# Mask rows of the second batch (batch one, counted from zero) by engine copies instead of DMAs, a selector made on GpSimd, and a new order of all work, in a fused block-sparse attention and SoLU feed-forward kernel

## The chip, the cores and the metric

The kernel runs on one core of a Trainium2 chip. The metric is the device time of one execution in microseconds; the time before is the median of three runs. A core has five engines with queues of their own: TensorE (PE, with PEld for its weight loads), VectorE (DVE), ScalarE (ACT), GpSimd (POOL) and SyncE (SP, which here issues nearly all DMAs). Each works through its own row of instructions in order and waits on semaphores for the others.

## The reference

Attention with a block mask over 4 batches, 8 heads, 768 positions and 64 columns per head; its output, as 3072 tokens of 512, goes through a feed-forward layer of width 1024 with a SoLU activation and a layer norm.

```python
scores = scale * np.matmul(q, k.transpose(0, 1, 3, 2))
mask = np.abs(blk_i - blk_j) <= 1          # blocks of 32
mask = mask | (blk_i == 0) | (blk_j == 0) | (blk_i == 23) | (blk_j == 23)
mask[qb rows, kb columns] = True           # for the 3 sampled blocks kb of each block row qb
attn = softmax(np.where(mask, scores, -1e9))
x = np.matmul(attn, v)                     # 3072 x 512, heads side by side
h = x @ w_in                               # 3072 x 1024
solu = h * softmax(h)
out = ((solu - mu) / np.sqrt(var + 1e-06) * g_ln) @ w_out
```

## The kernel before

Heads are taken in pairs (`pr`, 4 per batch). For each batch `b`, `kT` and `qT` hold k and q transposed: 64 rows of values and, below them, 24 **mask rows** (`MC = slice(64, 88)`). On k's side these say to which of the 24 blocks a key belongs, on q's side they hold minus 30000 for each block that a query may not see, so that one matmul of 88 rows gives the masked score. There are two buffers of each, for even and odd batches. The mask rows are the same for every batch and pair, and are made once.

*Opening.* Batch zero's k and q are loaded, cast (`cast2` to `cast6`), transposed on TensorE into `abank` (`turned`) and evacuated; its mask rows come along in the same transposition, from columns that affine selects (`own`) and small operations on VectorE (`bar`, ending in `bar_b`) have written. The **selector** `selp` (24 x 768) is block membership transposed: six transpositions on TensorE (`selp_tp`) and one copy on ScalarE (`selp`); with it `mask2` and `mcol` place `bar_b` in q's mask. For batch one, two DMAs (`m1dma`) copy all four pairs of mask rows from `kT[0]` and `qT[0]` to `kT[1]` and `qT[1]`, 288 KB each. They wait for all evacuations and for all casts of `w_in` (`castw`), because `w_in` is staged in the memory of `kT[1]` and `qT[1]`.

*Later batches.* `crossed` casts k and q (into `kb`, `qb`), transposes them by DMA (`cross_kq`, into `kx`, `qx`, shown as `kc` and `qx`) and **splits** the result by head into `kT` or `qT` with two copies of 64 rows each.

*Attention.* `attend(b, t, pr)` works on 256 queries and two heads: three groups of four score matmuls (L561) into one of two `sbank` buffers, each followed by one exponential of 128 x 1024 on ScalarE (L568), then 24 matmuls with `va` (L581) into one of two `mbank` buffers, a reciprocal (L590) and a normalisation (L593) into `x`.

*Feed-forward.* For each of 24 tiles of 128 tokens: x is transposed by DMA (`cross_x`) or on TensorE, 8 matmuls with `w_in` (L643), exponential with its sum (L666), product (L669), statistics (L676, L679), `u` transposed by DMA (`cross_u`), 8 matmuls with `w_out_sb` (L759), and scaling by `rs` (L767, L769). `rs` comes from three small operations on GpSimd (`z2` L682, `vr` L685, `rs` L718). `w_out` is prepared once: eight scalings by g (`wg`, L439), their column sum on TensorE (`cs`), `wbar` on ScalarE (L451) and eight products on VectorE (`wo`, L453).

*Order.* Nothing is scheduled at run time. The functions only list operations with what they depend on. `ORDER`, a list of numbers, gives the sequence in which all are issued and so each engine's row; `ENGINES` moves single operations of choice (casts, splits, scalings) to another engine. `SPARES` lists matmuls on constants (L823) that compute nothing that is used; they are placed by `ORDER` as well.

## Time and profile before

| | |
|---|---|
| median of 3 runs | 211.07 us (210.95 to 211.72) |
| profiled execution, its own time | 210.25 us |
| its span, first to last instruction | 208.5 us |
| busy TensorE / VectorE / ScalarE / GpSimd | 200.3 / 138.8 / 179.4 / 84.2 us |
| first score matmul, first exponential | 8.03, 8.67 us after the start |
| first score of batch one | 49.28 us |
| data moved by DMA | 43.19 MB |

The profiled execution is a single one and 0.8 us below the median. A busy TensorE is not a TensorE at its peak: neighbouring matmuls overlap, and the shown length of one is longer than its place in the row. In the rows "idle before" names the time in which an engine stood before this instruction, and "<-" what ended it.

### The profile page before, as it was taken

What the parts mean: (1) busy time and instruction counts of PE and PEld (TensorE: products, weight loads), DVE (VectorE), ACT (ScalarE), POOL (GpSimd) and SP (SyncE); (2) the same over time, 40 slices, a digit from 0 to 9 for tenths busy, and PEclk for the clock granted to TensorE, in tenths of its full rate; (3) what the DMA queues carried; (4) which work ended last, traced back from release to release, by engine and by line L of the source; (5) the groups of instructions that cost most, each with busy time, mean ns of one, the idle gap of its engine ahead of it and who ended that gap; (6) DMA issues with size and microseconds to landing.
All of it is one profiled execution on the core that took longest, in us unless ns stands there. A gap on an engine that the chain in (4) does not pass through costs nothing.

```text
span 208.5 us, 5748 instructions
## 1 busy us (share of the span) xinstructions
PE 200.3 (96%) x2282; PEld 142.0 (68%) x2313; DVE 138.8 (67%) x306; ACT 179.4 (86%) x230; POOL 84.2 (40%) x158
## 2 busy tenths in 40 slices
PE   8999999999999999999799999999999999999993
PEld 4798876756667768566566767666767758666452
DVE  5586689999887555757676864754755565485840
ACT  3599999998999999999599998989989898876683
POOL 4235398185540647316640731683320211001271
PEclk9999999999999999999999999999999999999999
DMA  5999995999999998999899989995393314672534
GB/s 142 336 358 347 384 361 123 205 226 287 211 222 327 311 189 208 254 263 286 230 299 228 233 185 251 207 257 126 101 127 99 63 19 104 151 105 53 122 134 152
DMA packets 71736, 43.19 MB, mean 207 GB/s; under 512 B 53348, under 2 KB 67180, under 8 KB 71660
## 3 DMA queue, kind: packets, MB, share of 16 engines
q1 hardware_dynamic: 71672, 42.81, 84.9%
q8 instruction: 18, 0.29, 0.6%
q14 instruction: 10, 0.08, 0.1%
q10 hardware_dynamic: 36, 0.00, 0.0%
HBM read 23.07 MB, written 6.29 MB: 141 GB/s over the span
## 4 chain that ended last, share of the span: by engine, by line
PE 73%; DVE 12%; DMA 7%; ACT 3%; issue 2%; SPq 1%; ACTq 0%
PE sbank L561 22%; PE mbank L759 15%; PE hbank L643 14%; PE mbank L581 13%; DMA qx<-qb 4%; DVE w_out_sb L453 3%; PE abank L477 3%; ACT ex L568 2%; DMA xT<-x 2%; DVE u L669 2%; PE tbank L643 2%; PE sbank L823 2%; DVE x L593 1%; DMA out_dram<-ot 1%; DVE w_in_sb L295 1%
## 5 line engine op out<-in xcount | busy, mean ns | idle before, releaser
L568 ACT ACTIVATE ex<-sbank 128x1024 bf16<-128x1024 f32 x144 | 141.0, 1025 | 15.7 <-PE sbank L561 14.2
L561 PE MATMUL sbank<-qT,kT 88*128 88x256 bf16 x576 | 81.5, 272 | 0.5 <-DVE qT L295 0.3
L561 PEld LDWEIGHTS <-kT 88*128 88x128 bf16 x576 | 52.7, 97 | 19.2 <-issue 0.9
L759 PE MATMUL mbank<-w_out_sb,uT 128*128 128x512 bf16 x175 | 45.0, 379 | 0.8 <-DVE w_out_sb L453 0.3
L581 PEld LDWEIGHTS <-ex 128*128 128x128 bf16 x1152 | 40.8, 97 | 7.0 <-issue 1.3
L581 PE MATMUL mbank<-va,ex 128*128 128x65 bf16 x1152 | 42.3, 193 | 1.4 <-DVE x L593 1.3
L643 PE MATMUL hbank<-w_in_sb,xT 128*128 128x512 bf16 x157 | 41.9, 378 | 1.4 <-DMA xT<-x 0.3
L669 DVE TENSOR_TENSOR u<-hbank,e 128x1024 bf16<-128x1024 f32 x22 | 26.8, 1216 | 19.6 <-ACT e L666 15.7
L676 DVE BATCH_NORM_STATS2 bs<-u 128x6 f32<-128x512 bf16 x44 | 29.2, 679 | 0.2
L643 PEld LDWEIGHTS <-xT 128*128 128x128 bf16 x192 | 18.2, 97 | 15.0 <-DMA xT<-x 0.8
L759 PEld LDWEIGHTS <-uT 128*128 128x128 bf16 x184 | 17.6, 97 | 14.6 <-issue 0.8
L590 DVE RECIPROCAL r<-mbank 128x4 f32<-128x4 f32 x48 | 8.3, 175 | 25.7 <-PE mbank L581 25.5
L666 ACT ACTIVATE e<-hbank 128x1024 bf16<-128x1024 f32 x22 | 22.5, 1024 | 1.3 <-PE hbank L643 1.3
L685 POOL TENSOR_SCALAR vr<-z,mv 128x1 f32<-128x1 f32 x22 | 5.8, 266 | 39.0 <-DVE mv L679 38.0
L593 DVE TENSOR_TENSOR x<-mbank,r 128x256 bf16<-128x256 f32 x48 | 19.7, 415 | 0.8
L718 POOL TENSOR_TENSOR rs<-vr,neg_half 128x1 f32<-128x1 f32 x24 | 13.8, 579 | 0.8
L295 POOL COPY qT<-kc 64x768 bf16<-64x768 bf16 x10 | 8.9, 889 | 11.7 <-DMA kc<-qb 6.1
L769 DVE TENSOR_SCALAR ot<-mbank,rs 128x512 f32<-128x512 f32 x13 | 9.7, 745 | 5.7 <-PE mbank L759 3.1
L682 POOL TENSOR_TENSOR z<-z 128x1 f32<-128x1 f32 x22 | 4.7, 212 | 20.1 <-ACT e L666 19.7
L295 POOL CAST kb<-kst 128x768 bf16<-128x768 f32 x7 | 6.2, 892 | 15.3 <-DMA kst<-in_k_dram 8.8
L295 POOL COPY kT<-kc 64x768 bf16<-64x768 bf16 x13 | 11.0, 844 | 2.6 <-DMA kc<-kb 2.2
L295 POOL CAST va<-vst 128x768 bf16<-128x768 f32 x8 | 6.6, 827 | 7.4 <-DMA vst<-in_v_dram 7.3
(110 smaller groups left out, 165.5 us busy)
## 6 DMA issues: line engine op xcount, KB each, us to landing
vst<-in_v_dram SPq DMA_DIRECT2D x16, 384.0 KB, 5.0
out_dram<-ot SPq DMA_DIRECT2D x23, 256.0 KB, 2.4
kst<-in_k_dram SPq DMA_DIRECT2D x15, 384.0 KB, 4.7
qst<-in_q_dram SPq DMA_DIRECT2D x12, 384.0 KB, 5.3
w_out_f<-in_moe_w_out_dram SPq DMA_DIRECT2D x2, 1024.0 KB, 8.4
qst<-in_q_dram SPq DMA_DIRECT2D x4, 256.0 KB, 5.9
kT<-in_moe_w_in_dram SPq DMA_DIRECT2D x2, 512.0 KB, 5.5
qT<-in_moe_w_in_dram SPq DMA_DIRECT2D x2, 512.0 KB, 9.4
```

Of the source, the lines that this page charges most:

```text
L295: (nc.vector if o.eng == "DVE" else nc.gpsimd).tensor_copy(out=dst, in_=src)
L561: nc.tensor.matmul(s[:, m, :], kT[i][0:KR, pr, jc, hh, :], qT[i][0:KR, pr, 2 * t : 2 * t + 2, hh, :], start=(m % 2 == 0), stop=(m % 2 == 1))
L568: exs.append(op("exp", "ACT", lambda o, so=so: nc.scalar.activation(out=exb[o.slot], in_=sbank[so.slot], func=ACT.Exp, scale=scale), [so], ...
L581: nc.tensor.matmul(acc(o)[:, qt, hh, :], exb[exs[n].slot][:, m, qt * P : (qt + 1) * P], va[i][:, 2 * pr + hh, jc, :], start=first, stop=(n ...
L593: nrm = op("norm", "DVE", lambda o: nc.vector.tensor_tensor(out=xb[x_of[b, t].slot][:, :, 2 * pr * D : (2 * pr + 2) * D].rearrange("p a (h ...
L643: nc.tensor.matmul(d, xTb[xt[0].slot][:, qt, c, :], w_in_sb[n][:, c, :], start=(c == 0), stop=(c == KD - 1))
L666: zs = op("silu_e", "ACT", lambda o: nc.scalar.activation(out=eb[o.slots["e"]], in_=hb(), func=ACT.Exp, accum_out=zb[o.slots["z"]][:, 0:1] ...
L669: us = op("mult", "DVE", lambda o: nc.vector.tensor_mul(out=ub[o.slot], in0=hb(), in1=eb[zs.slots["e"]]), [zs], take="u", last_of=[(hs[0], ...
L676: bs.append(op("stats", "DVE", lambda o, n=n: nc.vector.bn_stats(out=bsb[(bs[0] if bs else o).slot][:, n, :], in_=ub[us.slot][:, w(o, n)]) ...
L718: rs = op("rs", "POOL", lambda o: nc.gpsimd.tensor_tensor(out=rsb[o.slot], in0=vrb[vr.slot], in1=neg_half, op=ALU.pow), [vr, c2], take="rs ...
L759: nc.tensor.matmul(mbank[m0.slot], uTb[ut[0].slot][:, KF // 2 * n + f, :], w_out_sb[n][:, f, :], start=(n == 0 and f == 0), stop=(n == 1 a ...
L769: nc.vector.tensor_scalar(out=otb[o.slot], in0=mbank[os_[0].slot], scalar1=rsb[rs.slot], scalar2=None, op0=ALU.mult)
```

## The change

- `selp_tp` and its copy go. Four affine selects on GpSimd write `selp` directly, in two parts (two of the six chunks, then four).
- The two `m1dma` go. In their place stand eight copies `mrow` of 24 x 1536, one for each pair of k and q, on GpSimd or VectorE; each waits only for batch zero's first pair and for the casts of that part of `w_in` that lies in its place (`staged`). The splits of batch one wait for the same part instead of all of `w_in`.
- `kown` becomes in part an order (`after`) instead of a dependence. `iota_f`, `samp_f`, and of the feed-forward `z2` and `vr`, may now run on another engine.
- `SPARES`, `ENGINES` and `ORDER` are new throughout.

```diff
 SPARES = (
-    (512, 'a'), (256, 'a'), (128, 'm'), (512, 'a'), (512, 'a'), (512, 'm'), (512, 'a'), (512, 'm'), (256, 'm'),
...
+    (512, 's'), (512, 's'), (512, 's'), (512, 's'), (512, 's'), (128, 's'), (128, 's'), (128, 's'), (128, 's'),
...
-    st = op("selp_tp", "PE", selp_tp, [own, mids], take="m")
-    sels = op("selp", "ACT", lambda o: copy(
-        o, selp.rearrange("a c p -> a (c p)"), mbank[st.slot].bitcast(BF16)[0:NB, 0 : NCH * P]), [st], last_of=[st])
+    sels = []
+    for c0, c1 in ((0, 2), (2, NCH)):
+        a = op(f"selp{c1 - c0}", "POOL", lambda o, c0=c0, c1=c1: nc.gpsimd.affine_select(
+            out=selp[:, c0:c1], in_=nc.const_aps.tensor(1.0, (NB, c1 - c0, P), BF16), compare_op=ALU.is_ge,
+            fill=0.0, base=c0, channel_multiplier=-BLK, pattern=[[1, c1 - c0], [NCH, P]]))
+        sels.append(op(f"selp{c1 - c0}", "POOL", lambda o, c0=c0, c1=c1: nc.gpsimd.affine_select(
+            out=selp[:, c0:c1], in_=selp[:, c0:c1], compare_op=ALU.is_ge, fill=0.0, base=BLK - 1 - c0,
+            channel_multiplier=BLK, pattern=[[-1, c1 - c0], [-NCH, P]]), [a]))
...
-        [al, sels], take="m")
+        [al, sels[0]], take="m")
...
-    mc = op("mcol", "PE", mcol, [al, sels], take="m")
+    mc = op("mcol", "PE", mcol, [al] + sels, take="m")
...
-    w_in_b = w_in_n[0] + w_in_n[1]
+
+    def staged(nm, pr):
+        c0 = 0 if nm == "k" else 2
+        return [w_in_n[n][c0 + c] for c in ((0,), (0, 1), (1,), ())[pr] for n in range(2)]
+
...
-            got.append(op("split", "DVE", lambda o, hh=hh: copy(
+            got.append(op("split", "POOL", lambda o, hh=hh: copy(
                 o, dst[i][0:D, pr, :, hh, :], cx[t.slot][hh * D : hh * D + D]),
-                [t, last_use.get((b - 2, pr))] + (w_in_b if b == 1 else []), last_of=[t]))
-        got += ([mask1["k"]] if nm == "k" else [mask1["q"]]) if b == 1 else []
+                [t, last_use.get((b - 2, pr))] + (staged(nm, pr) if b == 1 else []), last_of=[t]))
+        got += [mask1[nm, pr]] if b == 1 else []
...
-            mask1["k"] = op("m1dma", "SP", lambda o: nc.sync.dma_start(out=kT[1][MC], in_=kT[0][MC]), kdone + w_in_b)
-            mask1["q"] = op("m1dma", "SP", lambda o: nc.sync.dma_start(out=qT[1][MC], in_=qT[0][MC]), qdone + mq0 + w_in_b)
+            for pr in range(NPR):
+                mask1["k", pr] = op("mrow", "POOL", lambda o, pr=pr: copy(
+                    o, kT[1][MC, pr], kT[0][MC, 0]), kdone[:2] + staged("k", pr))
+                mask1["q", pr] = op("mrow", "POOL", lambda o, pr=pr: copy(
+                    o, qT[1][MC, pr], qT[0][MC, 0]), [ready_q[0, 1, 0][0]] + mq0 + staged("q", pr))
```

What the engines' rows hold, at three places. Names are those of the tiles with their buffer numbers.

**The head, on GpSimd.** `kc0_80` takes the block membership, `ident_154` is the identity that every transposition on TensorE needs. Before:

```order
L307 AFFINE_SELECT kc0_80<-const-bfloat16-1.0 128x6x24
L461 MEMSET va1_66 128x48
L303 IOTA iota_d_170 24x24
L314 IOTA iota_k_169 24x24
L304 AFFINE_SELECT ident_154<-ident_154 128x128
L461 MEMSET va0_65 128x48
```

Now:

```order
L324 AFFINE_SELECT selp_181<-const-bfloat16-1.0 24x256
L304 IOTA iota_d_170 24x24
L314 IOTA iota_p_171 24x1
L308 AFFINE_SELECT kc0_80<-const-bfloat16-1.0 128x6x24
L311 AFFINE_SELECT kc0_80<-kc0_80 128x6x24
L465 MEMSET va1_66 128x48
L327 AFFINE_SELECT selp_181<-selp_181 24x256
L315 IOTA iota_k_169 24x24
L296 COPY kc0_80<-kc0_80 128x6x24
L324 AFFINE_SELECT selp_181<-const-bfloat16-1.0 24x512
L431 MEMSET onesf_152 128x128
L305 AFFINE_SELECT ident_154<-ident_154 128x128
```

The identity moved from the fifth place to the twelfth; three of the selector's four selects stand ahead of it, the fourth behind. On TensorE, 6272 columns of spare matmuls stand ahead of the first score before and now; behind it 4224 columns before, 896 now.

**From `wbar` to batch one's first score, on VectorE.** `u` and `uT` belong to the first feed-forward tiles; `kT1_62` and `qT1_64` are batch one's. The row before, from the second product:

```order
L453 SCALAR_TENSOR_TENSOR w_out_sb0_144<-w_out_f0_146,g_sb_149,wbar_148 128x512 x2
L295 COPY uT0_111<-mbank1_156 128x1024
L453 SCALAR_TENSOR_TENSOR w_out_sb0_144<-w_out_f0_146,g_sb_149,wbar_148 128x512 x2
L669 TENSOR_TENSOR u1_109<-hbank0_718,e1_107 128x1024
L453 SCALAR_TENSOR_TENSOR w_out_sb1_145<-w_out_f1_147,g_sb_149,wbar_148 128x512
L590 RECIPROCAL r1_120<-mbank0_155 128x4
L295 CAST qb0_78<-qst0_70 128x768
L676 BN_STATS bs1_129<-u1_109 128x6
L593 TENSOR_TENSOR x2_102<-mbank0_155,r1_120 128x2x128
L453 SCALAR_TENSOR_TENSOR w_out_sb1_145<-w_out_f1_147,g_sb_149,wbar_148 128x512
L295 COPY kT1_62<-kc0_80 64x6x128
```

Now:

```order
L673 TENSOR_TENSOR u1_109<-hbank0_684,e1_107 128x1024
L457 SCALAR_TENSOR_TENSOR w_out_sb1_145<-w_out_f1_147,g_sb_149,wbar_148 128x512
L594 RECIPROCAL r0_119<-mbank1_156 128x4
L296 COPY kT1_62<-kc0_80 64x6x128
L457 SCALAR_TENSOR_TENSOR w_out_sb1_145<-w_out_f1_147,g_sb_149,wbar_148 128x512
L296 COPY qT1_64<-qx0_83 64x6x128
L597 TENSOR_TENSOR x2_102<-mbank1_156,r0_119 128x2x128
L457 SCALAR_TENSOR_TENSOR w_out_sb1_145<-w_out_f1_147,g_sb_149,wbar_148 128x512
L296 COPY qT1_64<-qx0_83 64x6x128
L680 BN_STATS bs0_128<-u0_108 128x6
L296 COPY qT1_64<-kc2_82 64x6x128
L296 COPY qT1_64<-qT0_63 24x1536
```

Splits of batch one now stand between the last products, and the `q` mask row of its first pair (the last row) stands behind them on VectorE; that row and the splits are what the first score of batch one waits for.

**Batch two's preparation, on VectorE and SP.** Before, on VectorE, where `qb0_78` is the buffer for batch three's first q, freed by a DMA transposition, and `qT0_63<-kc2_82` the split of batch two's third pair:

```order
L590 RECIPROCAL r0_119<-mbank0_155 128x4
L295 CAST qb0_78<-qst0_70 128x768
L679 BN_AGGR mv3_133<-bs0_128 128x2
L593 TENSOR_TENSOR x1_101<-mbank0_155,r0_119 128x2x128
L590 RECIPROCAL r1_120<-mbank1_156 128x4
L593 TENSOR_TENSOR x1_101<-mbank1_156,r1_120 128x2x128
L295 COPY qT0_63<-kc2_82 64x6x128
```

Now, on VectorE, from the output scaling `ot1_116`, to the cast of batch three's first k into `kb1_77`:

```order
L780 TENSOR_SCALAR ot1_116<-mbank1_156,rs0_138 128x512
L594 RECIPROCAL r1_120<-mbank0_155 128x4
L683 BN_AGGR mv2_132<-bs0_128 128x2
L296 CAST qb0_78<-qst1_71 128x768
L597 TENSOR_TENSOR x0_100<-mbank0_155,r1_120 128x2x128
L296 CAST qb1_79<-qst0_70 128x768
L673 TENSOR_TENSOR u0_108<-hbank0_684,e0_106 128x1024
```

```order
L296 CAST va0_65<-vst1_74 128x12x64
L597 TENSOR_TENSOR x0_100<-mbank0_155,r1_120 128x2x128
L296 COPY kT0_61<-kc1_81 64x6x128
L686 TENSOR_TENSOR z21_135<-z1_122 128x1
L296 CAST kb1_77<-kst0_67 128x768
L296 COPY kT0_61<-kc0_80 64x6x128
```

and on SP, where the transposition out of `kb1_77` that frees it stands right behind the store of `ot1_116`:

```order
L377 DMA vst1_74<-in_v_dram 128x2x384
L784 DMA out_0_dram<-ot3_118 128x512
L377 DMA kst1_68<-in_k_dram 128x2x384
L784 DMA out_0_dram<-ot1_116 128x512
L537 DMA_TRANSPOSE kc0_80<-kb1_77 128x6x128
```

Batch three's casts of q stand far behind the transposition that frees their buffer now; the cast of its first k stands close behind one.

More of the change, by code (lines that the diff above doesn't have):

```diff
@@ L22 @@
     "POOL": [
[L23 to L24 removed]
+        9,
     ],
     "ACT": [
[L27 removed]
+        10, 22, 28, 31, 32, 101, 128, 407, 416, 614, 851, 888, 1026, 1041, 1057, 1077, 1079, 1081, 1104, 1127, 1130,
     ],
     "DVE": [
[L30 to L31 removed]
[4 rows of a table added]
     ],
@@ L319 @@
     kheld = [own1] + kown[1:]
-    def selp_tp(o):
-        d = mbank[o.slot].bitcast(BF16)
-        for c in range(NCH):
-            nc.tensor.matmul(d[0:NB, c * P : (c + 1) * P], kc[0][:, c, 0, MC], ident, is_transpose=True,
-                             start=(c == 0), stop=(c == NCH - 1))
-    st = op("selp_tp", "PE", selp_tp, [own, mids], take="m")
-    sels = op("selp", "ACT", lambda o: copy(
-        o, selp.rearrange("a c p -> a (c p)"), mbank[st.slot].bitcast(BF16)[0:NB, 0 : NCH * P]), [st], last_of=[st])
+    sels = []
[6 more added lines that the diff above has]
+            channel_multiplier=BLK, pattern=[[-1, c1 - c0], [-NCH, P]]), [a]))
     d2 = op("small", "DVE", lambda o: nc.vector.tensor_tensor(out=dist, in0=iota_d, in1=iota_d, op=ALU.mult),
@@ L340 @@
     static = op("small", "DVE", lambda o: nc.vector.memset(bar[1][:, 0 : NB : NB - 1], 0.0), [b1])
-    iof = op("small", "DVE", lambda o: nc.vector.tensor_copy(out=iota_f, in_=iota_k), [ik])
-    slo = op("small", "DVE", lambda o: nc.vector.tensor_copy(out=samp_f, in_=samp_i[:, :, 0]), [samp_dma])
+    iof = op("conv", "DVE", lambda o: copy(o, iota_f, iota_k), [ik])
+    slo = op("conv", "DVE", lambda o: copy(o, samp_f, samp_i[:, :, 0]), [samp_dma])
     prev, dep = bar[1], [static, iof, slo]
@@ L465, in cast_v @@
         i = b % 2
-        ready_v[(b, pr)] = op("cast6", "POOL", lambda o: copy(
+        ready_v[(b, pr)] = op("cast6" if b == 0 else "castb", "POOL", lambda o: copy(
             o, va[i][:, 2 * pr : 2 * pr + 2, :, 0:D], vst[ld.slot]),
@@ L470, with turned @@
     a_ops = []
-    def turned(pr, src, held, s0, c0, c1, dst, deps, eng, release=(), rows=KR):
+    def turned(pr, src, held, s0, c0, c1, dst, deps, eng, release=(), rows=KR, after=()):
         n = c1 - c0
@@ L478, in tp @@
                                  ident, is_transpose=True, start=(k == 0), stop=(k == 2 * n - 1))
-        t = op(f"turn{2 * n}", "PE", tp, deps + [mids], take="a", last_of=release)
+        t = op(f"turn{2 * n}", "PE", tp, deps + [mids], take="a", last_of=release, after=after)
         a_ops.append(op(f"evac{2 * n}", eng, lambda o: copy(
@@ L499, in opening @@
             gq = turned(pr, qa, cq, 0, 0, 2, qT[0], [cq], "DVE", [cq], rows=D)
-            ga = turned(pr, kc, ck, 0, 0, 2, kT[0], [ck] + kown, "ACT", [ck])
+            ga = turned(pr, kc, ck, 0, 0, 2, kT[0], [ck, kown[0]], "ACT", [ck], after=kown)
             gb = turned(pr, kc, ck, 2, 2, 6, kT[0], [cr], "DVE", [ck] + kheld)
@@ L508, in opening @@
             gq = turned(pr, qa, cq, 0, 0, 2, qT[0], [cq] + qown, "DVE", [cq])
-            ga = turned(pr, kc, ck, 0, 0, 4, kT[0], [ck] + kown, "DVE", [ck] + kheld)
+            ga = turned(pr, kc, ck, 0, 0, 4, kT[0], [ck, kown[pr % NKC]], "DVE", [ck] + kheld, after=kown)
             gb = turned(pr, kc, ck, 4, 4, 6, kT[0], [ck], "DVE", [ck] + kheld)
@@ L530, in crossed @@
         st, cb, cx, dst = (kst, kb, kx, kT) if nm == "k" else (qst, qb, qx, qT)
-        ca = op("cast6", "POOL", lambda o: copy(
+        ca = op("castb", "POOL", lambda o: copy(
             o, cb[o.slot], st[ld.slot].rearrange("p h c d -> p c h d")), [ld], take=nm + "b", last_of=[ld])
```

18 lines of the change are left out of this document (9 added, 9 removed), and 116 rows, old and new, of tables (ENGINES, ORDER, SPARES).

## The prediction

> **What bounds the kernel now.** I read the page first (busy shares, slices, chain), then the busy time by stretch, then single rows where the chain leaves TensorE. Of the page:
>
> ```profile
> span 208.5 us, 5748 instructions
> ...
> PE 200.3 (96%) x2282; PEld 142.0 (68%) x2313; DVE 138.8 (67%) x306; ACT 179.4 (86%) x230; POOL 84.2 (40%) x158
> ...
> PE 73%; DVE 12%; DMA 7%; ACT 3%; issue 2%; SPq 1%; ACTq 0%
> ```
>
> TensorE is the bound, ScalarE stands close behind, and the chain leaves TensorE for VectorE and DMA for a fifth of the span. The stretches say where (start and end, length, busy time of TensorE, its weight loads, VectorE, ScalarE and GpSimd with the number of instructions, the granted clock, the DMA share, GB/s):
>
> ```profile
> 8.00:20.00 12.00, 11.94 (x172) 10.61 (x171) 8.87 (x23) 10.71 (x12) 5.46 (x10) 1.00 1.04 357
> 20.00:30.00 10.00, 9.87 (x167) 8.81 (x166) 6.89 (x19) 9.67 (x11) 5.91 (x5) 1.00 1.03 377
> 30.00:40.00 10.00, 9.79 (x106) 6.82 (x107) 9.90 (x20) 9.37 (x14) 5.77 (x6) 1.00 0.82 165
> 40.00:50.00 10.00, 9.44 (x99) 6.34 (x99) 9.97 (x16) 9.45 (x13) 6.78 (x10) 1.00 1.06 261
> ...
> 100.00:110.00 10.00, 8.47 (x96) 5.89 (x94) 6.80 (x15) 7.68 (x10) 4.78 (x9) 1.00 1.14 284
> ```
>
> From 8 to 50 us ScalarE is busy 39.2 of 42 us (10.71 + 9.67 + 9.37 + 9.45), and TensorE is kept busy partly with spare matmuls; from 30 to 50 VectorE is full (9.90 and 9.97 of 10). After that TensorE is full but for one hole near 100 us. So an edit is worth something in three places: before the first score, in ScalarE's pace to 50 us, and at the hole.
>
> **The change part by part.**
>
> *The head.* These rows of the timeline lead to the first score:
>
> ```profile
> 0.89 0.35 POOL L307 TENSOR_SCALAR_AFFINE_SELECT kc<-const-bfloat16-1.0 128x144 bf16<-128x144 bf16 x1 [0.40 <-POOLq L856]
> 1.18 0.32 POOL L461 MEMSET va<- 128x48 bf16 x1
> ...
> 5.37 0.58 PE L477 MATMUL abank<-ident,kc 128*88 128x128 bf16 x4
> ...
> 6.70 0.41 DVE L295 CAST qT<-mbank 24x256 bf16<-24x256 f32 x1 [0.28 <-PE mbank L350]
> ...
> 7.14 0.36 ACT L293 CAST qT<-mbank 24x256 bf16<-24x256 f32 x1 [1.35 <-DVE qT L295]
> ...
> 7.50 0.64 PE L477 MATMUL abank<-ident,kc 128*88 128x128 bf16 x8
> ...
> 8.03 0.60 PE L561 MATMUL sbank<-qT,kT 88*128 88x256 bf16 x4
> 8.18 0.69 DVE L295 COPY kT<-abank 88x1024 bf16<-88x1024 bf16 x1 [0.40 <-PE abank L477]
> 8.67 1.02 ACT L568 ACTIVATE ex<-sbank 128x1024 bf16<-128x1024 f32 x1 [0.69 <-PE sbank L561]
> ```
>
> The selector's six transpositions leave TensorE and its copy leaves ScalarE; in their place GpSimd runs four affine selects. 144 elements take 0.29 us from start to start (0.89 to 1.18), 2.0 ns each: estimated, 0.5 us for each pair of 256 elements, 1.0 for each of 512. In GpSimd's new row stand ahead of the identity: 0.5 + 0.5 + 1.0 for selects of the selector, 0.7 for the two of `kc`, and some 1.2 for iotas, memsets and a copy. So the identity is ready at 0.89 + 3.9 + 0.24, about 5.0, and no transposition starts before; until now the first one ran at 5.37, so this costs nothing against before. Behind it, with the rows' durations: q's turn of four to 5.4, the mask product and spares to 5.8, the turn of eight to 6.3; beside that the mask copies on ScalarE (0.36) and VectorE (0.41) to 6.5, then the evacuation of 0.69 on VectorE to 7.25. First score about 7.3 instead of 8.03: **-0.7 us**. Bounds: 7.1, if the mask copy is done before the turn, and 8.03, if the third DMA or the selects are later than worked out.
>
> *The opening, to the first score of batch one.* TensorE's order gives 36 scores and 36 exponentials ahead of it before and now. On ScalarE two copies leave this stretch and two casts enter (rows of the view by line):
>
> ```profile
> L293 ACT COPY xT<-mbank 128x256 bf16<-128x256 bf16 x3 | 1.1, 368 | 1.9 <-PE mbank L613 1.9
> L293 ACT COPY qT<-qx 64x768 bf16<-64x768 bf16 x1 | 0.8, 831 | 0.0
> L293 ACT CAST kb<-kst 128x768 bf16<-128x768 f32 x1 | 0.8, 823 | 0.0
> ```
>
> On TensorE,
>
> ```profile
> 49.28 0.60 PE L561 MATMUL sbank<-qT,kT 88*128 88x256 bf16 x4
> ```
>
> is the first score of batch one (the 37th, behind the second group of out products). The ScalarE rows make 2 x 0.82 - 0.37 - 0.83, about +0.4. In the same stretch TensorE now does one more product with v (11 instead of 10), and spare matmuls behind the first score fall from 4224 columns to 896. A product with v is 24 matmuls; in the chain two of them took 1.46 us, and four out matmuls of 512 columns 0.86:
>
> ```profile
> 59.53 0.86 PE mbank L759 x4
> ...
> 81.53 1.46 PE mbank L581 x48
> ```
>
> If ScalarE sets the pace, the spares were waits under another name and their removal is worth nothing; if TensorE does, it is worth 3328 columns at 2048 in 0.86 us, 1.4 us. ScalarE's 39.2 of 42 us is nearer to the first, so I take nothing for the spares, +0.4 for ScalarE, and **-0.7** for the extra product (0.73) that then no longer stands behind. Together with the head: -1.0.
>
> *The mask rows.* The two DMAs go, with a wait in SP's queue:
>
> ```profile
> L812 SPq EVENT_SEMAPHORE  x2: 28/4048/8069, 24.0 to 32.1; - x2
> ```
>
> The queue stood 8.07 us for all casts of `w_in`; the DMA share was 1.03 in 20 to 30 us and 0.82 in 30 to 40, so at most 1.8 us of transfer was lost, and TensorE did not wait for it. I cost the removal at 0 (bounds -1.8 and 0). The eight copies of 24 x 1536 are not in this trace. The nearest rows are the splits, half as long, here three that show port sharing too:
>
> ```profile
> 48.29 0.34 DVE L295 COPY kT<-kc 64x768 bf16<-64x768 bf16 x1
> 49.96 1.03 DVE L295 COPY kT<-kc 64x768 bf16<-64x768 bf16 x1
> ...
> 49.95 0.82 POOL L295 COPY kT<-kc 64x768 bf16<-64x768 bf16 x1
> ```
>
> So on VectorE a copy costs 0.34 (nothing for twice the elements) to 2.06 us (twice the blocked one), and I take 0.6; on GpSimd 0.82 to 1.64, and I take 1.6, since its copies grow with the elements. Five of the eight run on VectorE and three on GpSimd; the last of those that batch one's first pair needs, for `q`, stands on VectorE and is waited for directly.
>
> *The weights of `w_out`.* All eight scalings go to VectorE, and six of eight casts of `w_in` to GpSimd. The eight products that follow have two SBUF inputs, and they too differ by what runs beside them:
>
> ```profile
> L453 DVE SCALAR_TENSOR_TENSOR w_out_sb<-w_out_f,g_sb,wbar 128x512 bf16<-128x512 f32 x8 | 7.9, 1012 | 0.0
> ...
> 36.27 0.63 ACT L451 ACTIVATE wbar<-mbank 128x512 f32<-128x512 f32 x1
> ...
> 37.08 0.73 DVE L453 SCALAR_TENSOR_TENSOR w_out_sb<-w_out_f,g_sb,wbar 128x512 bf16<-128x512 f32 x1
> ...
> 47.10 1.26 DVE L453 SCALAR_TENSOR_TENSOR w_out_sb<-w_out_f,g_sb,wbar 128x512 bf16<-128x512 f32 x1
> ```
>
> `wbar` stands behind 26 exponentials on ScalarE as before, less the 0.37 copy and the head's 0.7: it ends near 36.27 + 0.63 - 1.07 = 35.8. The stretch from the first product to the end of the last, 37.08 to 48.36, took 11.3 us. In the new row a cast leaves it (0.5) and four splits (0.34 each, fence above) and a mask row (0.6) join it, up to the `q` mask row of batch one's first pair; with the products at 0.73 instead of 1.01 (-2.2) that makes 10.6, done at 46.4. The first score of batch one wants it at 49.28 - 0.3, about 49.0. Hidden, with 2.6 us to spare; without this cover it is the third rival.
>
> *The hole near 100 us.*
>
> ```profile
> 91.77 1.40 SPq L533
> ...
> 93.21 7.35 DMA qx<-qb
> 100.59 0.56 DVE qb L295
> ...
> 99.87 0.60 PE L561 MATMUL sbank<-qT,kT 88*128 88x256 bf16 x4
> 101.61 0.89 PE L581 MATMUL mbank<-va,ex 128*128 128x65 bf16 x24 [1.14 <-DVE x L593]
> 102.78 0.61 PE L561 MATMUL sbank<-qT,kT 88*128 88x256 bf16 x4 [0.28 <-DVE qT L295]
> ```
>
> A cast for batch three on VectorE waits for its buffer, until a transposition of 7.35 us lands, and holds up the normalisation and split behind it. TensorE needs 0.44 for a score group and 0.73 for the product, so it stands 1.30 + 0.44 = 1.74 us. In the new order that cast stands far behind the transposition that frees its buffer, and batch two's transpositions stand some 10 us of TensorE work further ahead of their scores: **-1.7** (bounds -1.7 and 0).
>
> *VectorE's extra load.* By the order's counts it gains 7 splits, 5 mask rows, 4 output scalings, 4 scalings of `w_out` and 23 operations on single columns, and gives off 5 casts of `w_in`, some casts of v and k, and part of its waits on the port. The two largest prices:
>
> ```profile
> L769 DVE TENSOR_SCALAR ot<-mbank,rs 128x512 f32<-128x512 f32 x13 | 9.7, 745 | 5.7 <-PE mbank L759 3.1 <-POOL z L682 1.9 <-POOL ss L705 0.4
> ...
> L295 DVE COPY kT<-kc 64x768 bf16<-64x768 bf16 x11 | 4.5, 408 | 1.3 <-DMA kc<-kb 1.2
> ```
>
> 7 x 0.41 + 4 x 0.75 + 5 x 0.6 make 9; I take the rest as cancelling. So VectorE goes from 138.8 to some 148 us, from 67% to 71%. It is hidden where VectorE has gaps; I charge **+0.5** (bounds 0 and 3). The tail has the same products in nearly the same order: 0, within 0.3.
>
> Sum: -0.7 + 0.4 - 0.7 - 1.7 + 0.5 = -2.2. The profiled execution took 210.25 with 208.5 of span, 0.8 below the median of 211.07; taken from the median this gives **208.9 us**.
>
> The Trainium skill, "SBUF — State Buffer", section "Who interferes with whom", says that VectorE and GpSimd share one pair of ports as an exclusive lock, held for a whole instruction, with the second one blocked fully. The trace agrees: 1.03 against 0.34 us. By that rule each 1.6 us mask copy on GpSimd can hold a product on VectorE for its whole length, which speaks against the change and is the third rival.
>
> **The rivals.**
>
> 1. *No change.* ScalarE paces the opening, the product gained is given back as a wait, and a new wait of about the old size takes the place of the hole. For it: ScalarE's 39.2 of 42 us. Against it: the hole had one cause, which the order moves. -0.7 + 0.4 from the opening, +0.5 for VectorE: 211.3, and with the extra product kept 210.5; say 210.2 to 211.9.
>
> 2. *Slower: VectorE's queue stands under a late transposition.* VectorE takes 25 of 48 splits instead of 18. The worst place is batch three's first cast of `k`, `kb1_77`, which stands 15 rows behind the output scaling whose store SP must issue before the transposition that frees the buffer. Those 15 rows (one multiplication, three casts, two splits, three norms and small ones) sum to an estimated 5.0 us. A transposition of the usual size is there in time:
>
> ```profile
> kc<-kb SPq DMA_TRANSPOSE x12, 4.3
> ```
>
> One like that of the hole takes 1.40 to issue and 7.35 to land, so VectorE stands 3.7 us, and TensorE with it once its two banks are used up: 208.9 + 3.7 = 212.6. It decides from 7.2 us of issue and landing on, since a wait under 2.2 only eats the gain. For it: the DMA share is above 1.0 in most stretches. Against: loads now come earlier, so that the queue should be shorter there.
>
> 3. *Slower: the port lock.* If GpSimd's mask copies and splits fall on the eight products, each takes the 1.26 of the blocked row, 0.53 more, and the mask row waits out one copy of 1.6: 5.8 late less 2.6 of cover, +3.2, or 212.1. For it: it happened to the products here. Against: GpSimd's row has a wait for ScalarE and for a landing between its copies.
>
> 4. *Faster than forecast.* TensorE paces the opening after all: the 1.4 for the spares counts and ScalarE's 0.4 does not, 208.9 - 1.8 = 207.1; with the DMA time that SP's wait cost given back as well (1.8), 205.3.
>
> **How the numbers follow.** Differences under 0.5% (1.06 us) can hardly be told from none here. Forecast 0.38, fourth rival 0.17, first 0.19, second 0.17, third 0.09. The forecast's own case spans 207.7 to 210.0, all faster by more than 0.5%: faster 0.55, same 0.19, slower 0.26. The range leaves out the lowest of the fourth rival and anything worse than the second's price: 206.2 to 212.8; the forecast's own range is the narrower one just given.
>
> **What would show it.** The head: first exponential near 7.9 instead of 8.67, the identity's select ending near 5.0. The opening: first score of batch one near 49.0 instead of 49.28. The weights: eight products under 0.8 us each, the last ending before 45 instead of 48.3. The hole: no wait of TensorE over 1 us between 90 and 110. Wrong: VectorE idle on a DMA with TensorE waiting for a norm or a split (second rival), products of 1.2 us beside GpSimd copies (third), or a first score still at 8 us because a load or the selects came late.

## The result and the profile after

The changed kernel takes **216.5 us** (median of four runs, 215.3 to 217.21) against 211.01 (210.86 to 211.72): a ratio of 1.0291, 95% interval 1.0243 to 1.034. It is slower by about 5.5 us where 2.2 less was predicted, and outside the predicted range. The profiled execution took 215.30 us with a span of 213.3 and a full granted clock; the other three had a granted clock of 0.984 to 0.992, which the last section takes up.

The page after, the same lines as the prediction showed of before:

```profile
span 213.3 us, 5743 instructions
...
PE 199.0 (93%) x2277; PEld 141.2 (66%) x2308; DVE 147.6 (69%) x342; ACT 177.3 (83%) x228; POOL 75.9 (36%) x135
...
PE 57%; DVE 16%; DMA 15%; SPq 5%; issue 3%; POOL 2%; ACT 1%; POOLq 0%; DVEq 0%
```

VectorE's load came out as worked out (147.6, "some 148"), but the chain now runs through TensorE for 57% of the span instead of 73%, and the DMA share of it has doubled. TensorE's waits, before (the first three rows there are) and after (engine, what the waiting instruction writes and its line, what it waited for; total us, times, longest):

```profile
PE mbank L581 <- DVE x L593: 1.3, 2, 1.1
PE sbank L823 <- PEq L856: 0.8, 1, 0.8
PE mbank L759 <- DVE w_out_sb L453: 0.3, 1, 0.3
```

```profile
PE hbank L647 <- DMA xT<-x: 3.3, 2, 1.7
PE mbank L770 <- DVE uT L296: 1.8, 1, 1.8
PE mbank L585 <- DVE ot L780: 1.1, 2, 0.8
...
PE hbank L647 <- DVE w_in_sb L296: 0.6, 1, 0.6
PE mbank L770 <- DMA uT<-u: 0.5, 1, 0.5
```

So TensorE, which stood for 1.3 us in the hole and hardly elsewhere, now stands for transpositions of `x` and `u` by DMA, and once for an evacuation on VectorE. Where this lies in time, in two stretches of before and then of after (columns as in the prediction: start and end, length, busy time of TensorE, its weight loads, VectorE, ScalarE, GpSimd, clock, DMA share, GB/s):

```profile
26.00:70.00 44.00, 43.00 (x509) 30.68 (x515) 39.42 (x76) 41.20 (x52) 24.78 (x32) 1.00 1.04 251
70.00:135.00 65.00, 62.76 (x716) 44.18 (x724) 41.85 (x87) 59.35 (x72) 29.32 (x51) 1.00 1.08 238
```

```profile
26.00:70.00 44.00, 39.89 (x464) 27.85 (x468) 40.19 (x84) 38.33 (x46) 19.67 (x25) 1.00 1.03 258
70.00:135.00 65.00, 60.13 (x692) 42.32 (x701) 43.44 (x99) 55.36 (x67) 25.94 (x38) 1.00 1.06 229
```

TensorE is idle 4.1 us instead of 1.0 from 26 to 70, and 4.9 instead of 2.2 from 70 to 135. (Not all of this is loss: spare matmuls count as busy, and the new order has fewer; see `fewer_spares`.) Of the prediction's shorter stretches, 40 to 50 us holds the largest part of the first, 1.3 of 3.1:

```profile
40.00:50.00 10.00, 8.11 (x90) 5.38 (x90) 9.81 (x21) 7.90 (x11) 1.42 (x2) 1.00 1.01 246
```

TensorE 8.11 instead of 9.44, with VectorE full as before. The timeline of VectorE and GpSimd in and just ahead of it, TensorE's wait, and batch one's first score (start, length, engine, line, operation):

```profile
36.24 2.04 DVE L457 SCALAR_TENSOR_TENSOR w_out_sb<-w_out_f,g_sb,wbar 128x512 bf16<-128x512 f32 x1 [0.35 <-ACT wbar L455]
...
38.75 3.88 DVE L457 SCALAR_TENSOR_TENSOR w_out_sb<-w_out_f,g_sb,wbar 128x512 bf16<-128x512 f32 x4
42.55 0.68 DVE L296 COPY uT<-mbank 128x1024 bf16<-128x1024 bf16 x1
...
44.28 0.73 DVE L457 SCALAR_TENSOR_TENSOR w_out_sb<-w_out_f,g_sb,wbar 128x512 bf16<-128x512 f32 x1
...
36.27 1.46 POOL L296 COPY kT<-kT 24x1536 bf16<-24x1536 bf16 x1
37.80 1.16 POOL L296 CAST kb<-kst 128x768 bf16<-128x768 f32 x1
38.91 1.27 POOL L296 COPY kT<-kc 64x768 bf16<-64x768 bf16 x1
40.14 1.27 POOL L296 CAST kb<-kst 128x768 bf16<-128x768 f32 x1
...
43.28 1.04 PE L770 MATMUL mbank<-w_out_sb,uT 128*128 128x512 bf16 x4 [1.82 <-DVE uT L296]
...
51.09 0.60 PE L565 MATMUL sbank<-qT,kT 88*128 88x256 bf16 x4
```

The first five products run beside GpSimd's mask copy, split and casts and take 2.04 and 0.97 us each; the last three, with GpSimd idle, 0.73 to 0.75. The evacuation of `uT` stands behind these five in VectorE's row, and TensorE waits 1.82 us for it. In sum the eight products are hardly slower than before (8.1 us against 7.9); but before, four of them stood ahead of the evacuation (2.8 us, 0.73 + 2.06) and the slow ones behind it, and now five do (5.9 us). The first score of batch one, the 37th group of four, starts at 51.09 us instead of 49.28. The later waits start in SP's queue (first fence) and end on TensorE (second):

```profile
73.72 0.57 SPq L377 DMA_DIRECT2D qst<-in_q_dram  x1
74.39 0.41 SPq L377 DMA_DIRECT2D kst<-in_k_dram  x1
74.91 1.23 SPq L627 DMA_TRANSPOSE xT<-x  x1
...
122.33 0.98 SPq L377 DMA_DIRECT2D vst<-in_v_dram  x2
123.36 0.47 SPq L377 DMA_DIRECT2D qst<-in_q_dram  x1
123.87 1.67 SPq L784 DMA_DIRECT2D out_dram<-ot  x1
125.65 1.39 SPq L627 DMA_TRANSPOSE xT<-x  x1
```

```profile
81.37 0.82 PE L647 MATMUL hbank<-w_in_sb,xT 128*128 128x512 bf16 x3 [1.56 <-DMA xT<-x]
...
131.44 0.82 PE L647 MATMUL hbank<-w_in_sb,xT 128*128 128x512 bf16 x2 [1.71 <-DMA xT<-x]
```

In both places loads, and once stores, were issued in the 4 us ahead of the transposition, and TensorE got the result 6.5 and 5.8 us after its issue.

### The profile page after: what moved, and what is told of

Its sections match the earlier page's. It is cut to its first block, busy times and chain, and to the rows that moved or that the text cites. A ratio compares the mean times of both kernels' runs of the same rounds, so it can differ in the third digit from the quotient of the medians.

```text
span 213.3 us, 5743 instructions
## 1 busy us (share of the span) xinstructions
PE 199.0 (93%) x2277; PEld 141.2 (66%) x2308; DVE 147.6 (69%) x342; ACT 177.3 (83%) x228; POOL 75.9 (36%) x135
## 4 chain that ended last, share of the span: by engine, by line
PE 57%; DVE 16%; DMA 15%; SPq 5%; issue 3%; POOL 2%; ACT 1%; POOLq 0%; DVEq 0%
PE sbank L565 17%; PE mbank L770 13%; PE hbank L647 12%; PE mbank L585 11%; DMA qst<-in_q_dram 3%; DVE w_out_sb L457 3%; DMA kc<-kb 3%; DMA uT<-u 3%; DVE bs L680 3%; DMA xT<-x 3%; DMA sq<-in_q_dram 2%; DVE qT L296 2%; DVE u L673 2%; SPq L377 2%; DVE kT L296 2%
## 5 line engine op out<-in xcount | busy, mean ns | idle before, releaser
L296 POOL COPY kT<-kc 64x768 bf16<-64x768 bf16 x15 | 13.8, 918 | 13.3 <-DMA kc<-kb 12.8
L780 DVE TENSOR_SCALAR ot<-mbank,rs 128x512 f32<-128x512 f32 x17 | 12.6, 740 | 2.6 <-POOL rs L729 1.4
L686 POOL TENSOR_TENSOR z<-z 128x1 f32<-128x1 f32 x13 | 2.5, 194 | 33.5 <-ACT e L670 33.4
L296 POOL CAST va<-vst 128x768 bf16<-128x768 f32 x10 | 8.6, 856 | 10.3 <-DMA vst<-in_v_dram 10.3
L695 POOL TENSOR_SCALAR vr<-z,mv 128x1 f32<-128x1 f32 x8 | 2.3, 283 | 21.2 <-DVE z L686 17.4
L457 DVE SCALAR_TENSOR_TENSOR w_out_sb<-w_out_f,g_sb,wbar 128x512 bf16<-128x512 f32 x8 | 8.1, 1045 | 0.4 <-ACT wbar L455 0.4
```

Source lines behind the costliest of these rows:

```text
L296: (nc.vector if o.eng == "DVE" else nc.gpsimd).tensor_copy(out=dst, in_=src)
L457: wo = [op("wo", "DVE", lambda o, c=c: (nc.vector if o.eng == "DVE" else nc.gpsimd).scalar_tensor_tensor(out=w_out_sb[c // 4][:, c % 4, :] ...
```

## The experiments

Ratios are to the kernel before, with 95% intervals; beside these runs the kernel before had medians of 209.4 to 210.1 us. A difference between two of these ratios is uncertain by 0.5 to 0.8 points (1.0 to 1.6 us). ENGINES and ORDER are the kernel's two tables, and an operation is told by its name. `kT` and `qT` mask copies of the changed kernel are called mask copies.

**again** is the changed kernel once more.

> The changed kernel itself once more, as the measure for the others. Theory 'holes': its time is 215.3 to 217.2 us with TensorE waits of 1.5 us and more near 43, 81, 103 and 131 us after the start, the same places as in its first profile. Rival 'clock': the granted clock lies under 1.0 in the longer executions, and time over the 213.3 us of span goes with the clock, not with the waits (0.984 with a span of 215.3, 0.992 with 214.5 to 214.8 so far).

215.56 us, 1.028 [1.0225, 1.0335]. The loss repeats, and so do the waits: 1.83 us at 43, 1.32 at 82, 0.76 at 104 and 1.80 at 132, with one more for `uT` (1.71 at 69). The clock does not order the executions: two at full clock took 215.99 and 217.95 us, four at 0.992 took 214.89 to 216.81.

**Which part costs.** `sel_only` is the kernel before with the selector made on GpSimd. `parts_old` adds the eight mask copies, two on GpSimd and six on VectorE, with the other operations in the order of before. `mask_dma` is the kernel after with the two mask DMAs back.

```diff
 sel_only, against before
-    six transpositions selp_tp (TensorE), copy selp (ScalarE)
+    four affine_select selp (GpSimd): two behind own_cp, two behind the last cast2
 parts_old, against sel_only
-    m1dma x2 (SP)
+    mrow x8: k0, q0, k2, q2, k3, q3 on VectorE; k1, q1 on GpSimd
 mask_dma, against after
-    mrow x8
+    m1dma x2 (SP), behind the casts of w_in
```

> Kernel before with the selector alone made by four affine selects on GpSimd, everything else in the order of before. If the selector by itself gives the head's gain: first exponential 0.3 to 0.8 us earlier than 8.67 and the time 0.2 to 0.8 us less (ratio 0.996 to 0.999). If the new order of the head gave it: first exponential within 0.2 us of 8.67, time the same.

> Both parts of the change (selector by four affine selects, mask rows by eight copies, six on VectorE and two on GpSimd) in the order of before, with the copies put in where their inputs are ready. If the parts are a gain and the new order lost it: 0.990 to 0.998, since two DMAs of 288 KB and the 8 us wait of SyncE's row go. If the copies themselves cost: VectorE, full from 30 to 50 us, makes TensorE wait for splits or the mask rows near 45 to 50 us, ratio 1.004 to 1.015.

> Changed kernel, but the mask rows of batch one again by the two DMAs of before (288 KB each) in place of the eight copies, all else in the new order. Theory 'parts' (the copies cost what was lost): the time falls by 2 us or more. Theory 'holes' (the order costs it): only the first product is freed (2.04 to about 0.9), and the time falls by 0 to 1.3 us; the waits near 81, 103 and 131 stay.

`sel_only` gives 209.05 us, 0.9979 [0.995, 1.0008]. Its first exponential starts at 7.65 us instead of 8.67. At the end the interval holds both no gain and a gain of 1.0 us, so that it cannot be said what this is worth. `parts_old` gives 212.14, 1.012 [1.0068, 1.0173]: 1.4 points above `sel_only`, 3.0 us. TensorE's busy time from 26 to 70 shows where, in `sel_only` and then in `parts_old`:

```profile
26.00:70.00 44.00, 43.12 (x519) 30.62 (x519) 38.47 (x77) 40.76 (x51) 24.24 (x33) 1.00 1.08 244
```

```profile
26.00:70.00 44.00, 39.94 (x461) 27.90 (x459) 40.76 (x74) 38.06 (x47) 25.02 (x31) 1.00 0.86 199
```

VectorE does 2.3 us more there and TensorE 3.2 less. TensorE's first waits in `parts_old` are all for work on VectorE:

```profile
PE mbank L442 <- DVE ex L433: 1.3, 1, 1.3
PE hbank L637 <- DVE u L663: 1.0, 1, 1.0
PE mbank L753 <- DVE w_out_sb L447: 0.9, 1, 0.9
```

So in the order of before, copies that keep VectorE busy for 3.9 us in all, put in place of two DMAs, cost 3.0 us (give or take 1.3) at the places that they were given. `mask_dma` gives 218.58, 1.037 [1.032, 1.042]: in the new order the copies are better than the DMAs, by 0.9 points, hardly more than the uncertainty. That does not price the copies alone, since a new wait came with the DMAs, 4.43 us for `xT` up to 46.9 us, and a spell of half clock behind it (last section).

**The hole.** `hole_before` is the kernel before with the cast that made the hole (batch three's `q`) moved behind the norms and the split that it held up; `sel_hole` is the same with the selector.

```diff
 hole_before, ORDER, VectorE's row
-    cast6 (waits for its buffer), norm x2, split, norm
+    norm x2, split, norm, cast6
```

> Kernel before, with one cast moved: batch three's cast of q on VectorE, which waited for the 7.35 us transposition near 100 us, stands behind the four normalisations of that tile. By the prediction's term the hole of 1.7 us goes: 0.8 to 1.7 us less, ratio 0.992 to 0.996. Rival: TensorE finds the next late thing (a split or a transposition) and the time stays within 0.4 us.

> Kernel before with the selector on GpSimd and the moved cast of batch three's q together. If the two gains hold side by side: ratio 0.990 to 0.996, faster than the kernel before and the best version so far. If what they free is taken back by the next late transposition: 0.996 to 1.001.

209.49 us, 0.9998 [0.9971, 1.0025], and 209.45, 0.9992 [0.9964, 1.0019]. The wait is gone (TensorE's waits in `hole_before`), and nothing is gained:

```profile
PE hbank L642 <- DMA xT<-x: 1.1, 1, 1.1
PE sbank L822 <- PEq L855: 0.8, 1, 0.8
```

The wait for `xT` is no answer to the edit: it stands at 78.41 us, and the edit moves one instruction near 100. Nor did every execution of the old order have the hole. In `sel_only` and `fewer_spares` the same cast stands at the same place of VectorE's row, and it starts without a wait for its buffer (98.92 and 100.95 us); TensorE stands no more than 0.3 us there. So the hole was in one of three traces.

**The spare matmuls.** `fewer_spares` takes 3328 columns of spare matmuls from behind the first score of the kernel before.

```diff
 spare matmuls behind the first score, columns
-    4224
+    896
```

> Kernel before without ten of the spare matmuls behind the first score (3328 columns, as many as the change takes away there). If ScalarE paces the opening: the same time within 0.4 us. If TensorE does: 1.0 to 1.4 us less (ratio 0.993 to 0.995). If the spares hold the clock up: longer, with a granted clock under 1.0 between 10 and 50 us.

209.62 us, 0.9991 [0.9951, 1.0031]. The spares were waits under another name; a gain of 1.4 us (0.9933) lies outside the interval. From 26 to 70 us TensorE is idle 2.0 us in this kernel instead of 1.0, at the same time at the end; so up to 1 us of the 3.1 more idle in the changed kernel there can be missing spares and no loss.

**The traffic.** `half_after` and `half_before` load half of each k and v pair of batches one to three (192 KB instead of 384, 24 loads), with all instructions in place; what is left out stays as an earlier load left it, so that the output is not the reference's.

```diff
-        load(..., src[b, 2 * pr : 2 * pr + 2]...)
+        n = 1 if b and which in "kv" else 2
+        load(..., src[b, 2 * pr : 2 * pr + n]...)
```

> Changed kernel, leaving out half of each load of k and v for batches one to three (192 instead of 384 KB, 24 loads, 4.6 of 42.6 MB); the other head's data are those of an earlier load. Theory 'transfers' (transpositions of x and u are late because loads and stores stand ahead of them): TensorE's waits for them (3.8 and 5.1 us in the two profiles) fall under 1.5 us in sum, the wait near 43 us stays, and the time falls by 2.5 to 4 us, to 1.008 to 1.018 of the kernel before. Rival 'lead' (the order leaves too little work between, whatever is loaded): the waits stay above 2.5 us and the time is the same within 0.8 us.

> Kernel before, with the same halves of the loads of k and v left out: the measure for the run on the changed kernel. Theory 'transfers': it has one such wait (the hole of 1.7 us near 100 us), so it falls by 1 to 2 us only, to 0.990 to 0.996. If it falls by as much as the changed kernel, the loads cost both orders alike and are no reason for the difference.

211.27 us, 1.0083 [1.0055, 1.0112], and 208.06, 0.9932 [0.9894, 0.9971]. Fewer bytes are worth 2.0 points to the new order and 0.7 to the old one; so 1.3 of the 2.8 points, some 2.7 us (give or take 1.5), need the full traffic. The stretches of `half_after`:

```profile
26.00:70.00 44.00, 40.73 (x469) 28.14 (x466) 39.42 (x85) 38.53 (x47) 20.67 (x26) 1.00 0.92 216
70.00:135.00 65.00, 64.19 (x750) 45.25 (x748) 45.51 (x106) 59.48 (x72) 26.83 (x39) 1.00 0.91 189
```

From 70 to 135 us TensorE's idle time falls from 4.9 to 0.8 (in the old order from 2.2 to 0.2), and what is left of the waits for `xT` is 0.2 us. From 26 to 70 it falls only from 4.1 to 3.3 (in the old order 1.0 to 1.2), and the first score of batch one stays late, at 50.97 us against 49.40 in `half_before`. What is left, 1.0083 against 0.9932 or 1.5 points (3.2 us), so lies mainly in that first stretch.

**What delays a transposition.** `x_first` moves loads (and one store) behind the two late transpositions. `dose` and `dose2` put rising numbers of transfers ahead of three late transpositions of `x`: 384 KB loads from HBM, and copies of 256 KB within SBUF. Their destinations are not read again.

```diff
 x_first, ORDER, SP's queue
-    load q, load k, xT<-x            load v, load v, load q, store, xT<-x
+    xT<-x, load q, load k            xT<-x, load v, load v, load q, store
 dose, against after
+    1, 2, 3 loads ahead of three transpositions of x
 dose2, against after
+    1, 2, 4 copies of x into kst ahead of the same three
```

> Changed kernel, with two transpositions of x issued ahead of the loads (and one store) that stand right before them in SyncE's row. Theory 'queue': the two waits of TensorE for x transposed (1.56 us near 81, 1.71 near 131) fall under 0.5 us each, and the time falls by 2 to 3 us. Rival 'late norm': x is normalised too late or the transposition lands late all the same; the waits stay above 1.2 us and the time is the same within 0.7 us.

> Changed kernel with extra loads of 384 KB that nobody uses, right ahead of three transpositions of x in the quiet last quarter: one, two and three loads ahead of those issued at 154.0, 171.7 and 183.6 us, which landed 3.0, 3.2 and 3.2 us after their issue. Theory 'transfers': 0.7 to 1.2 us later for each load, so about 4, 5 and 6.5 us. Rival (transpositions do not mind loads ahead; it is SyncE's row or late inputs): all three stay within 3.0 to 3.5 us.

> Changed kernel with extra copies of 256 KB right ahead of three transpositions of x in the quiet last quarter; they copy x itself, so that they are issued when the transposition could be: one, two and four copies. Theory 'transfers': the landing goes from 3.0 to 3.2 us up to about 3.7, 4.4 and 6 us, and TensorE waits for the last one for 2 us or more. Theory 'clock': behind a wait of over 2 us the granted clock falls under 1.0 for some microseconds; behind shorter ones it does not. Rival: landing within 3.0 to 3.5 us in all three.

`x_first` gives 218.7 us, 1.042 [1.038, 1.046]. The waits for `xT` fall to 0.4 us, as meant, but the loads then stand nearer to other transpositions, and `uT` is the late one. The longest wait is for one that was issued at 132.7 us, 4 us behind the loads and right behind two transpositions of k, and took 5.2 us:

```profile
PE mbank L770 <- DMA uT<-u: 4.7, 3, 3.0
```

The doses tell less than meant. In `dose` (a single execution, 217.71 us) SP ran ahead, so that only the three loads stood right before their transposition; it landed in 5.0 us instead of 3.2, and TensorE waited. SP's queue and TensorE in `dose`:

```profile
183.88 1.48 SPq L846 DMA_DIRECT2D qst<-in_k_dram  x3
185.47 1.23 SPq L627 DMA_TRANSPOSE xT<-x  x1
...
190.52 1.68 PE L647 MATMUL hbank<-w_in_sb,xT 128*128 128x512 bf16 x7 [1.99 <-DMA xT<-x]
```

In `dose2` (a single execution, 217.97) one, two and four copies gave landings of 3.2, 3.3 and 3.4 us: here copies within SBUF did not do what the loads did.

**The blocked products.** Four edits of the kernel after free VectorE's products from GpSimd. `clear5` gives GpSimd's three mask copies and a split to VectorE and two of its casts to ScalarE; `early3` moves a cast and two mask copies on GpSimd ahead of work for batch zero; `port` moves two mask copies earlier still, and the split and one cast off GpSimd. `half_clear5`, `half_early3` and `half_port` are these with the halved loads, so that late transpositions do not hide a gain.

```diff
 clear5, ENGINES
-    POOL: mrow x3, split kT, castb x2
+    DVE: mrow x3, split kT; ACT: castb x2
 early3, ORDER, GpSimd's row
-    z2, castb, mrow, mrow
+    castb, mrow, mrow, z2
 port, ORDER and ENGINES
-    POOL: mrow, ..., mrow, mrow, castb, split kT, castb
+    POOL: mrow, mrow, mrow, ..., castb; DVE: split kT; ACT: castb
```

> Changed kernel, with the five GpSimd operations that run beside the products of w_out moved away: three mask copies and one split to VectorE, two casts of k to ScalarE. Theory 'port': the eight products take 0.73 us each (now 2.04, and 3.88 for the next four), TensorE's wait of 1.8 us for uT near 43 us goes, and the time falls by 1.0 to 2.0 us. Rival 'load': the products stay above 1 us on average, or VectorE's extra 2 us and ScalarE's extra 1.7 us eat the gain, and the time stays within 0.5 us or grows.

> Changed kernel with both suspected costs taken away: the five GpSimd operations beside the products of w_out moved off, as in clear5, and half of each load of k and v for batches one to three left out, as in half_after. If port and transfers are all that the new order lost: no wait of TensorE over 1 us anywhere, and 1.5 to 2.5 us less than half_after (ratio 1.0083), so 0.996 to 1.001, within 0.5% or so of half_before (0.9932). Rival: a third cost is in the order; the ratio stays above 1.004.

> Changed kernel, with three GpSimd operations (the mask copies of pair one for k and q, and the cast of q behind them) moved ahead of the small operation that made GpSimd stand 7.0 us for ScalarE; nothing is added to VectorE or ScalarE. Theory 'port': the first product falls from 2.04 to 0.73 us, the first five from 5.9 to 3.7 to 4.7 us, TensorE's wait of 1.8 us near 43 falls under 0.8, and the time falls by 0.7 to 1.8 us, if the transfers behind do not take it back. Rival: the products stay slow (sum over 5.5), or they are faster and the time stays within 0.5 us, since the next late transposition takes the gain.

> The same move together with half of each load of k and v for batches one to three left out, so that late transpositions cannot take the gain. Theory 'port and transfers': 1.0 to 2.0 us less than half_after (ratio 1.0083), so 0.998 to 1.004. Rival: within 0.003 of 1.0083; then what is left between the orders is neither the products nor the transfers.

> The same moves in the changed kernel with its full loads. Theory 'port' alone: 1 to 2 us less than the changed kernel (1.028), so 1.019 to 1.023. Theory 'transfers take it back': TensorE is earlier by 2 us at 45 us, and the waits for transpositions behind it grow by as much; ratio 1.025 to 1.031.

> Changed kernel with half of each load of k and v for batches one to three left out, and GpSimd's copies kept off the products by the least that does it: the two mask copies of pair one moved right behind the earlier one (GpSimd stood idle there), one split to VectorE (0.34 us), one cast of k to ScalarE (0.83 us). Theory 'port and transfers': the products take 0.73 to 0.75 us each, the wait near 43 us (1.8) goes, and the time is 1.0 to 2.0 us less than half_after (ratio 1.0083): 0.998 to 1.004. Rival: products at 0.75 and the time within 0.003 of 1.0083; then freeing the products only lets TensorE reach the next late thing sooner, and the products carry nothing of the loss.

| kernel | median us | ratio | TensorE busy, 26 to 70 us |
|---|---|---|---|
| after, again | 215.56 | 1.028 [1.0225, 1.0335] | 39.89 (after) |
| clear5 | 221.08 (216.75 to 221.97) | none | 37.66 |
| early3 | 215.21 | 1.0254 [1.0196, 1.0311] | 41.04 |
| port | 218.03 | 1.0361 [1.0302, 1.0421] | 37.79 |
| half_after | 211.27 | 1.0083 [1.0055, 1.0112] | 40.73 |
| half_clear5 | 213.46 | 1.0176 [1.0123, 1.0229] | 38.65 |
| half_early3 | 211.85 | 1.0125 [1.0058, 1.0191] | 39.65 |
| half_port | 211.86 | 1.0097 [1.006, 1.0134] | 39.84 |

Five of six executions of `clear5` had a granted clock of 0.974 to 0.984 and no ratio is given; the sixth, at full clock, took 216.75. Its trace has two pauses of TensorE of over 2 us, each with half clock behind it. `clear5` and `port`, with and without the full loads, did free the products; `early3` and `half_early3` hardly did (0.98 and 0.89 us each). The group of eight by line, after and then in `half_port` (busy us, mean ns of one):

```profile
L457 DVE SCALAR_TENSOR_TENSOR w_out_sb<-w_out_f,g_sb,wbar 128x512 bf16<-128x512 f32 x8 | 8.1, 1045 | 0.4 <-ACT wbar L455 0.4
```

```profile
L449 DVE SCALAR_TENSOR_TENSOR w_out_sb<-w_out_f,g_sb,wbar 128x512 bf16<-128x512 f32 x8 | 5.7, 742 | 0.0
```

Each takes 0.74 us instead of 1.05, in `port`, `clear5` and `half_clear5` too. None of the kernels is faster for it beyond the intervals. Other waits came up; TensorE's in `half_port`:

```profile
PE mbank L762 <- DMA uT<-u: 2.4, 2, 1.3
PE hbank L639 <- DVE w_in_sb L287: 1.5, 1, 1.5
PE mbank L577 <- DVE x L589: 0.6, 2, 0.3
```

The mask copies that left the products now run beside VectorE's casts of `w_in`, for which TensorE waits 1.5 us; in `half_clear5`, three mask copies on VectorE hold up a normalisation, and TensorE waits 1.4 us for it. That kernel has the opening back, with the first score of batch one at 49.15 us, and loses it again to waits of about 1 us each for two splits on GpSimd (at 52 and 67 us) and of 1.95 us at 57 for a small operation on VectorE. The blocked products are real, and freeing them is not enough to win the loss back.

## Why the prediction was wrong

It foresaw 208.9 us, faster; the kernel is slower, beyond the second rival's 212.6. By its steps:

- **The head, right, in part by luck.** The first score starts at 7.13 us (7.3 foreseen) and the first exponential at 7.78 (7.9), by the end of the path that was given: mask copies to 6.36, then the evacuation. Its start was another: the identity's select ends at 3.99, not 5.0, and the first transposition waits for a copy on ScalarE, to 4.64. The selects cost 0.62 us for 512 elements and 0.40 for 256, where 1.0 and 0.5 were estimated. `sel_only` had 1.0 us here and no gain at the end that can be told from nothing.
- **The spares at nothing, right,** by `fewer_spares`.
- **The prices of the mask copies, nearly right.** VectorE 0.55 (0.6 taken) in four of five and 1.28 in the one that was blocked, GpSimd 1.46 (1.6).
- **The opening and the weights of `w_out`, wrong: "with the products at 0.73 instead of 1.01".** They took 1.05, since GpSimd's mask copy, its split and its casts run beside the first five. The last ended at 47.5 us, not before 45. This is the third rival's mechanism, but the mask row was in time (it ended at 49.5) and what came late was the evacuation of `uT`, which the rival did not name. The first score of batch one starts at 51.09 us, where 49.0 was foreseen; TensorE's waits ahead of it are 1.82 us for `uT`, 0.63 for a cast of `w_in` (at 28.07, behind the one blocked mask copy) and 0.37 for a normalisation. The 11 products with v were ahead of it as foreseen.
- **The hole, wrong by its worth.** TensorE's longest wait from 90 to 110 us is 0.75, as foreseen. But "-1.7" took a wait of one profiled execution for a fixed part of the time. `sel_only` and `fewer_spares` do not have it, and `hole_before`, which takes it away, gives 0.0 with an interval of 0.6 us either side.
- **VectorE's load, wrong by size: "+0.5, hidden where VectorE has gaps".** The prediction's own rows had VectorE at 9.90 and 9.97 of 10 us from 30 to 50, where the splits and one mask copy were added; two more stand just ahead. `parts_old` prices copies at 3.0 us in the old order, a figure at the bound that was given (3).
- **No term for the transpositions of `x` and `u`.** The second rival asked only whether a late transposition holds up a cast of `k`, and took "loads now come earlier" as relief. The loads came right ahead of the transpositions that TensorE feeds on. By the halved loads this is 2.7 of the 5.9 us (2.8 points of 210), give or take 1.5.

Shown: the loss repeats; some 2.7 us of it need the full load traffic, mostly between 70 and 135 us in waits for transpositions; the selector costs nothing that can be measured, and the copies cost 3.0 us in the old order. The other 3.2 us are only located, mainly from 26 to 70 us, where TensorE waits on VectorE's row and batch one's first score comes 1.8 us late. That they are the same 3.0 us of copies is plausible by place and size, but not shown: what freed the products, or took the copies away, brought other waits. Loads dated differently for all transpositions at once were not tried.

No kernel here that does the whole work beats the one before measurably; `sel_only` comes nearest.

## What to carry to other kernels

Price an addition to an engine's row by its full length in any stretch where the stretch's row shows that engine full, whatever its share of the whole span. When an order is changed, list for each DMA that the bound engine waits for what now stands ahead of it in its queue, and halve the loads in both orders to see what that is worth. Count a wait as a cost only when more than one execution has it: profile a kernel with the same rows a second time before an edit is priced by a hole. And count a wait removed as a gain only when the next wait behind it has been looked for.
